# Moving steps and V loads inside the blocks of a fused windowed-attention and SwiGLU kernel, and splitting its last store

## The chip, the core and the metric

The kernel runs on one core of one Trainium2 chip. The metric is the device time in microseconds of one execution, as the median of several runs. TensorE (PE) multiplies matrices and writes PSUM; VectorE (DVE), ScalarE (ACT) and GpSimd (POOL) do the elementwise work; GpSimd also issues most loads, and SyncE (SP) issues the stores and the transposing DMAs. Each engine works through its own list of instructions in order and waits on semaphores for the others.

## What is computed

Attention over 4 batches, 8 heads, 768 positions and a head dimension of 64, in which a query sees the first 8 keys (global) and the 96 keys up to itself (local), with a bias that falls linearly with distance; then a SwiGLU feed-forward over the 3072 tokens, from 512 to 1536 features and back:

```python
scores = scale * np.matmul(q, k.transpose(0, 1, 3, 2))
keep = is_global | is_local
scores = np.where(keep, scores + bias, -1e9)          # bias = -slope_h * distance
a = softmax(scores)
x = np.matmul(a, v)                                   # -> tokens x 512
g = x @ w_gate
out = (g * sigmoid(g)) * (x @ w_val) @ w_out          # float32
```

## The kernel before

Tokens are cut into 8 tiles of 384 (t = 0 to 7), two for each batch, and the 1536 hidden features into 12 slices of 128 (f = 0 to 11). For each (t, f) the feed-forward makes a **gate** group and a **value** group of four matmuls each (L477, `gps` and `vps`), whose results rotate through three PSUM banks. ScalarE takes tanh of half the gate (`th`, L488); VectorE forms `sl` = (th + 1) * gate (L490) and then `hT` = value * `sl` (L494). A bank is free again once `sl`, for a gate, or `hT`, for a value, has read it. The product with `wo` (L506, `ops`) of an earlier tile is cut into **output** groups of three matmuls, of which one is put behind most (t, f); after the fourth, ScalarE copies the 128 x 512 result to `osb` (L511) and SyncE stores it (L513).

The attention of the batch that comes next is put between these groups as **steps**. A step holds some of these:

- `sc(b, hp, bk)`: scores of one pair of heads and one bank of keys (L358), their exponentials on ScalarE (L367), and a multiplication by a mask that holds window and bias (L375, L378; on VectorE, on GpSimd for a few).
- `va(b, hp, half)`: denominators and numerators (`nd`, L406), a copy of the numerators (`ns`, L419), the inversion of the denominators on VectorE (`dT`, `dR`, `rb`, L422 to L427), and the scaled result `xT` (L434), on GpSimd from batch 1 on. `xT` is what the feed-forward reads.
- `fetch`: for batches 2 and 3, SyncE turns keys and queries of two pairs of heads by transposing DMAs (L446) into `kN` and `qT`. `sp` (`spread_keys`, L450) then copies `kN` to the key layout `kT` on VectorE (L454, L457, L458).

Work after the matmuls of a step is not emitted with it but put on the list `later`; one entry is taken off with each following group (L738), all of them before the next step (L745), and also all of them at f = 0 of a token tile (L737).

The steps are dealt out by a count. The program is cut into seven **stretches**; stretch 2 holds the first attention of batch 1, stretches 3 and 4 are the long blocks of two token tiles each (24 f), in which the second half of batch b and the first of batch b + 1 are done in 11 steps, and stretch 5 holds the rest of batch 3. Every group adds its weight (1 for gate or value, 1.1 for output), times a quota, to a debt; when the debt reaches 1, a step is emitted:

```python
        work = sum(g[0] for g in groups)
        quota = len(steps) / (work - (1.0, 0, 5.0, 3.0, 3.0, 4.5, 3.0)[n])
        owed = -0.1 if n == 0 else 0.4
```

The larger the number taken off `work`, the earlier all steps of the stretch come.

Loads of queries, keys and values for later batches are issued by GpSimd, one by one, at places given as 12 t + f (`at_step`, L695). For batches 2 and 3 they are `load_rows` (L196: 16 loads of keys and queries for each batch) and then `load_v_rest` (L171: 7 chunks c of values). Chunks 0 to 3 are read by the first half of a batch's `va`, chunks 3 to 6 by the second.

Of the kernel before, what the change touches and what calls it, by code (L numbers as in the profile page):

```python
# [9 lines left out]
FP32 = mybir.dt.float32  # L10
# [27 lines left out]
def kernel(  # L38
# [12 lines left out]
    nc = tc.nc  # L51
# [7 lines left out]
    DM = H * D  # L59
    DFF = moe_w_gate.shape[1]  # L60
    NFF = DFF // 128
    NC = DM // 128
    J = S // 128
    NCH = 7
# [26 lines left out]
    sb2 = ctx.enter_context(tc.tile_pool(name="sb2", bufs=2))  # L91
# [16 lines left out]
    for hp in range(2):  # L108
        for st, src in ((k32, k), (q32, q)):
            nc.sync.dma_start(  # L110
                out=st[:, 2 * hp:2 * hp + 2, :],
                in_=src[0, 2 * hp:2 * hp + 2, 0:TB, :].rearrange(
                    "h (p j) d -> p h (j d)", p=128))
# [29 lines left out]
    for j in range(J2):  # L143
        nc.vector.tensor_copy(
            out=perm[:, j, :, NG + j::J2],
            in_=identx.rearrange("p (c m) -> p c m", c=NC0))
        n = (NG - j + J2 - 1) // J2
        nc.vector.tensor_copy(
            out=perm[:, j, :, j:NG:J2],
            in_=identx[:, 0:n].unsqueeze(1).broadcast_to([128, NC0, n]))  # L150
# [18 lines left out]
    def load_v_rest(b, c):  # L169
        n = min(KC, S - KC * c)  # L170
        nc.gpsimd.dma_start(  # L171
            out=vSs[b][NG:NG + n, c, :, :],
            in_=v[b, :, KC * c:KC * c + n, :].rearrange("h p d -> p h d"))
# [16 lines left out]
    def stage_rows(b):  # L190
        qst[b] = sb2.tile([128, NP, J, 2, D], FP16, name="qst", tag="qst")
        kst[b] = sb2.tile([128, NP, J, 2, D], FP16, name="kst", tag="kst")

    def load_rows(b, i, h):
        st, src = ((qst[b], q), (kst[b], k))[i]
        nc.gpsimd.dma_start(  # L196
            out=st[:, h // 2, :, h % 2, :],
            in_=src[b, h].rearrange("(t p) d -> p t d", p=128))
# [37 lines left out]
    def single(name, tag, dt=FP32):  # L236
        return ps.tile([128, 512 if dt == FP32 else 1024], dt, name=name, tag=tag)
# [8 lines left out]
    def run_later(n):  # L246
        for _ in range(n):
            if later:
                later.pop(0)()
# [232 lines left out]
    def gate_or_val(t, f, which, c0=0):  # L482
        products(t, f, which, c0, NC)
        dst = gv.pop((f, which))

        if which == 0:
            th = sb2.tile([128, TB], FP32, name="th", tag="th")
            nc.scalar.activation(out=th, in_=dst[:, 0:TB], func=AF.Tanh, scale=0.5)  # L488
            sl = sb2.tile([128, TB], FP32, name="sl", tag="sl")
            nc.vector.scalar_tensor_tensor(  # L490
                out=sl, in0=th, scalar=1.0, in1=dst[:, 0:TB], op0=AluOp.add, op1=AluOp.mult)
            gv["sl"] = sl
        else:
            nc.vector.tensor_mul(hTs[t][:, f, :], dst[:, 0:TB], gv["sl"])  # L494
# [3 lines left out]
    def out_part(t, i, part):  # L498
        if part == 0:
            if t == NT - 1 and i < 2:  # L500
                ops_t[0] = single("ops", f"a{i}")
            else:
                ops_t[0] = single("ops", "o0")
        ops = ops_t[0]
        for f in range(3 * part, 3 * part + 3):
            nc.tensor.matmul(  # L506
                ops, lhsT=hTs[t][:, f, 128 * i:128 * i + 128], rhs=wo[:, f, :],
                start=(f == 0), stop=(f == NFF - 1))
        if part == 3:
            osb = sb2.tile([128, DM], FP32, name="osb", tag="osb")  # L510
            nc.scalar.mul(out=osb, in_=ops, mul=0.5)  # L511
            r0 = TB * t + 128 * i
            nc.sync.dma_start(out=out[r0:r0 + 128, :], in_=osb)  # L513


    NT = TOK // TB
# [178 lines left out]
    def at_step(t, f, *fns):  # L695
        loads.setdefault((t, f), []).extend(fns)
# [12 lines left out]
        at_step(0 if c < 2 else 1, (10 + c) % 12, lambda c=c: load_v_rest(1, c))  # L709
    for c in range(4, NCH):  # L710
        at_step(1, 2 * c - 1 if c < 6 else 10, lambda c=c: load_v_rest(1, c))
    for b, base, rate in ((2, 23, 2.0), (3, 43, 1.4)):
        items = [lambda b=b: stage_rows(b)]
        for hp in range(NP):
            for i in (1, 0):
                for hi in range(2):
                    items.append(lambda b=b, i=i, h=2 * hp + hi: load_rows(b, i, h))
        items += [lambda b=b, c=c: load_v_rest(b, c) for c in range(NCH)]
        for n, it in enumerate(items):
            at_step((base + int(n / rate)) // NFF, (base + int(n / rate)) % NFF, it)  # L720

    outs = [(t, i, part) for t in range(NT - 1) for i in range(3) for part in range(4)]
    for n, (tiles, steps) in enumerate(stretches):
        groups = []
        for t, f, n_out in tiles:
            for which in range(0 if f is None else 2):
                groups.append((0.05 if t == 0 and f < 2 else 1.0, t, f, which))
            groups += [(1.1, t, f, 2)] * n_out
        work = sum(g[0] for g in groups)
        quota = len(steps) / (work - (1.0, 0, 5.0, 3.0, 3.0, 4.5, 3.0)[n])  # L730
        owed = -0.1 if n == 0 else 0.4
        for w, t, f, which in groups:
            if which == 0:
                for ld in loads.pop((t, f), []):
                    ld()
                if f == 0:
                    run_later(len(later))  # L737
            run_later(1)  # L738
            if which == 2:
                out_part(*outs.pop(0))  # L740
            else:
                gate_or_val(t, f, which, NC if t == 0 and f < 2 else 0)
            owed += w * quota
            while owed >= 1.0 and steps:
                run_later(len(later))  # L745
                for step in steps.pop(0):
                    step()
                owed -= 1.0
        assert not steps
    assert not later and not loads and not outs  # L750
    for i in range(3):
        for part in range(4):
            out_part(NT - 1, i, part)
# [35 lines left out]
```

## Time and profile before

| | |
|---|---|
| time, median of 3 runs (lowest, highest) | 263.62 us (263.35, 264.06) |
| span of the profiled execution | 262.0 us |
| `th` on ScalarE, `sl` and `hT` on VectorE, one each | 495, 547, 546 ns |
| `xT` on GpSimd, one | 1001 ns |
| V load, issue on GpSimd, one | 888 ns |
| exponentials of 432 columns, one | 538 ns |
| `osb`, one | 598 ns |

The page gives busy time by engine, then the chain of waits that ended last, then the groups of instructions by line. Busy time says which engine is nearest to full; the chain says whose work was last at each moment; the timeline, which lists instructions with their start and duration, says where an engine had to wait, and for whom. For TensorE, whose matmuls overlap, the distance from one start to the next tells more than the busy time.

### The profile page before, as it was taken

What the parts mean: (1) busy time and instruction counts of PE and PEld (TensorE: products, weight loads), DVE (VectorE), ACT (ScalarE), POOL (GpSimd) and SP (SyncE); (2) the same over time, 40 slices, a digit from 0 to 9 for tenths busy, and PEclk for the clock granted to TensorE, in tenths of its full rate; (3) what the DMA queues carried; (4) which work ended last, traced back from release to release, by engine and by line L of the source; (5) the groups of instructions that cost most, each with busy time, mean ns of one, the idle gap of its engine ahead of it and who ended that gap; (6) DMA issues with size and microseconds to landing.
All of it is one profiled execution on the core that took longest, in us unless ns stands there. A gap on an engine that the chain in (4) does not pass through costs nothing.

```text
span 262.0 us, 5568 instructions
## 1 busy us (share of the span) xinstructions
PE 246.9 (94%) x2144; PEld 140.4 (54%) x2144; DVE 184.1 (70%) x422; ACT 134.7 (51%) x296; POOL 100.8 (38%) x117
## 2 busy tenths in 40 slices
PE   7787899899999999899999999999999999999993
PEld 5464455465655566445555566455565565555541
DVE  6378689967777677987876668977966559656510
ACT  4465687559873564455633653556534643332321
POOL 9663662100236956901338876801111223300000
PEclk9999999999999999999999999999999999999999
DMA  6999999980155999990059996991011101101122
GB/s 164 170 198 166 186 204 203 195 54 3 45 73 62 123 163 112 168 152 13 29 73 79 152 168 60 123 158 43 0 40 44 40 3 40 40 3 40 40 83 80
DMA packets 81010, 24.82 MB, mean 95 GB/s; under 512 B 66832, under 2 KB 77912, under 8 KB 80984
## 3 DMA queue, kind: packets, MB, share of 16 engines
q0 software_dynamic: 63264, 13.83, 60.1%
q1 hardware_dynamic: 17720, 10.64, 18.6%
q8 instruction: 17, 0.28, 0.4%
q14 instruction: 9, 0.07, 0.1%
HBM read 28.63 MB, written 6.29 MB: 133 GB/s over the span
## 4 chain that ended last, share of the span: by engine, by line
PE 68%; DVE 13%; DMA 8%; ACT 4%; issue 3%; POOL 2%; POOLq 0%; DVEq 0%; ACTq 0%
PE ops L506 20%; PE vps L477 19%; PE gps L477 18%; DMA q<-in_q_dram 8%; PE nd L406 6%; PE sc L358 3%; DVE sl L490 3%; DVE hT L494 2%; DVE rb L427 2%; DVE dT L422 2%; ACT at L367 2%; PE trs L262 1%; ACT th L488 1%; DVE dR L423 1%; POOL k L116 1%
## 5 line engine op out<-in xcount | busy, mean ns | idle before, releaser
L488 ACT ACTIVATE th<-gps 128x384 f32<-128x384 f32 x94 | 46.5, 495 | 67.1 <-PE gps L477 63.6
L490 DVE SCALAR_TENSOR_TENSOR sl<-th,gps 128x384 f32<-128x384 f32 x94 | 51.4, 547 | 40.0 <-ACT th L488 39.6
L477 PE MATMUL vps<-xT,wv 128*128 128x384 f16 x376 | 76.6, 326 | 2.0 <-DVE sl L490 1.6
L477 PE MATMUL gps<-xT,wg 128*128 128x384 f16 x376 | 77.0, 327 | 1.3 <-DVE hT L494 0.8
L506 PE MATMUL ops<-wo,hT 128*128 128x512 f16 x288 | 75.7, 380 | 0.0
L434 POOL TENSOR_TENSOR xT<-ns,rb 128x384 f16<-128x384 f32 x24 | 24.0, 1001 | 95.9 <-DVE rb L427 91.9
L494 DVE TENSOR_TENSOR hT<-vps,sl 128x384 f16<-128x384 f32 x94 | 51.3, 546 | 6.9 <-PE vps L477 0.6
L477 PEld LDWEIGHTS <-wg 128*128 128x128 f16 x384 | 36.1, 98 | 34.7 <-issue 3.8
L477 PEld LDWEIGHTS <-wv 128*128 128x128 f16 x384 | 36.0, 98 | 28.5 <-issue 5.1
L506 PEld LDWEIGHTS <-hT 128*128 128x128 f16 x288 | 26.9, 98 | 24.9 <-issue 0.9
L367 ACT ACTIVATE at<-sc 128x432 f16<-128x432 f32 x72 | 33.0, 538 | 3.7 <-PE sc L358 3.7
L171 POOL DMA_DIRECT2D vS<-in_v_dram x25 | 22.1, 888 | 7.6 <-DMA wo<-in_moe_w_out_dram 4.9
L511 ACT ACTIVATE osb<-ops 128x512 f32<-128x512 f32 x24 | 14.4, 598 | 19.8 <-PE ops L506 19.8
L419 ACT COPY ns<-nd 128x384 f32<-128x384 f32 x28 | 13.4, 478 | 17.2 <-PE nd L406 16.4
L427 DVE STREAM_TRANSPOSE rb<-dR 128x384 f32<-128x384 f32 x32 | 18.1, 568 | 0.9
L378 DVE TENSOR_TENSOR at<-at,masks 128x864 f16<-128x864 f16 x20 | 14.4, 720 | 3.4 <-ACT at L367 3.2
L422 DVE STREAM_TRANSPOSE dT<-nd 128x384 f32<-128x384 f32 x28 | 16.1, 573 | 0.3 <-PE nd L406 0.3
L343 ACT ACTIVATE at<-sc 128x432 f16<-128x432 f32 (+2 forms) x32 | 11.9, 444 | 5.8 <-PE sc L335 5.8
L406 PEld LDWEIGHTS <-ones 128*64 128x64 f16 x288 | 10.9, 110 | 7.3 <-issue 6.8
L196 POOL DMA_DIRECT2D kst<-in_k_dram x16 | 13.7, 874 | 0.0
L196 POOL DMA_DIRECT2D qst<-in_q_dram x16 | 13.7, 867 | 0.0
L406 PE MATMUL nd<-at,ones 128*64 128x216 f16 (+6 forms) x256 | 13.2, 231 | 0.0
(77 smaller groups left out, 190.1 us busy)
## 6 DMA issues: line engine op xcount, KB each, us to landing
out_dram<-osb SPq DMA_DIRECT2D x24, 256.0 KB, 2.1
vS<-in_v_dram POOLq DMA_DIRECT2D x21, 120.0 KB, 6.7
wg<-in_moe_w_gate_dram POOLq DMA_DIRECT2D x6, 256.0 KB, 8.8
wv<-in_moe_w_val_dram POOLq DMA_DIRECT2D x6, 256.0 KB, 8.7
wo<-in_moe_w_out_dram POOLq DMA_DIRECT2D x3, 512.0 KB, 11.9
kst<-in_k_dram POOLq DMA_DIRECT2D x16, 96.0 KB, 4.2
qst<-in_q_dram POOLq DMA_DIRECT2D x16, 96.0 KB, 5.1
kst<-in_k_dram POOLq DMA_DIRECT2D x2, 384.0 KB, 15.0
```

Source lines behind the costliest of these rows:

```text
L171: nc.gpsimd.dma_start(out=vSs[b][NG:NG + n, c, :, :], in_=v[b, :, KC * c:KC * c + n, :].rearrange("h p d -> p h d"))
L196: nc.gpsimd.dma_start(out=st[:, h // 2, :, h % 2, :], in_=src[b, h].rearrange("(t p) d -> p t d", p=128))
L367: nc.scalar.activation(out=at[:, hi, :], in_=sc[hi][:, 0:BANK], func=AF.Exp, scale=scale)
L406: nc.tensor.matmul(dst[r, o:o + n], lhsT=ones[:, 0:64] if ones_side else vals[:, 2 * hp + hi, :], rhs=self.at[cb][:, hi, col:col + n], sta ...
L422: nc.vector.transpose(dT, den[:, 0:TB])
L427: nc.vector.transpose(rb.rearrange("p (n i) -> p n i", i=32), dR.unsqueeze(2).broadcast_to([128, TB // 32, 32]))
L434: mul_eng.tensor_mul(dst, src, rb)
L477: nc.tensor.matmul(gv[f, which][:, 0:TB], lhsT=w[:, c, 128 * f:128 * f + 128], rhs=x_of(t)[:, c, :], start=(c == 0), stop=(c == NC - 1))
L488: nc.scalar.activation(out=th, in_=dst[:, 0:TB], func=AF.Tanh, scale=0.5)
L490: nc.vector.scalar_tensor_tensor(out=sl, in0=th, scalar=1.0, in1=dst[:, 0:TB], op0=AluOp.add, op1=AluOp.mult)
L494: nc.vector.tensor_mul(hTs[t][:, f, :], dst[:, 0:TB], gv["sl"])
L506: nc.tensor.matmul(ops, lhsT=hTs[t][:, f, 128 * i:128 * i + 128], rhs=wo[:, f, :], start=(f == 0), stop=(f == NFF - 1))
```

## The change

It does three things. The loads of the values of batches 2 and 3 get places of their own: chunks 0 to 3 about where they were, chunks 4 to 6 behind the boundary between the two token tiles of a block, so that they do not lie with the work around it. The numbers taken off `work` grow in stretches 2 to 5, so that the attention steps end sooner in each block. And the last output tile is copied from PSUM in two halves, by ScalarE and VectorE, and stored by two queues, ScalarE's and SyncE's.

```diff
         if part == 3:
             osb = sb2.tile([128, DM], FP32, name="osb", tag="osb")
-            nc.scalar.mul(out=osb, in_=ops, mul=0.5)
             r0 = TB * t + 128 * i
-            nc.sync.dma_start(out=out[r0:r0 + 128, :], in_=osb)
+            if t == NT - 1 and i == 2:
+
+                oB = sb2.tile([128, DM // 2], FP32, name="osb", tag="th")
+                nc.scalar.mul(out=osb[:, 0:DM // 2], in_=ops[:, 0:DM // 2], mul=0.5)
+                nc.vector.tensor_scalar_mul(oB, ops[:, DM // 2:], 0.5)
+                nc.scalar.dma_start(out=out[r0:r0 + 128, 0:DM // 2], in_=osb[:, 0:DM // 2])
+                nc.sync.dma_start(out=out[r0:r0 + 128, DM // 2:], in_=oB)
+            else:
+                nc.scalar.mul(out=osb, in_=ops, mul=0.5)
+                nc.sync.dma_start(out=out[r0:r0 + 128, :], in_=osb)
...
-    for b, base, rate in ((2, 23, 2.0), (3, 43, 1.4)):
-        items = [lambda b=b: stage_rows(b)]
+    for b, base, rate, v_at in ((2, 24, 2.0, (30, 31, 32, 32, 37, 38, 39)), (3, 43, 1.4, (54, 55, 56, 57, 61, 62, 63))):
+        items = [(base, lambda b=b: stage_rows(b))]
+        n = 0
         for hp in range(NP):
             for i in (1, 0):
                 for hi in range(2):
-                    items.append(lambda b=b, i=i, h=2 * hp + hi: load_rows(b, i, h))
-        items += [lambda b=b, c=c: load_v_rest(b, c) for c in range(NCH)]
-        for n, it in enumerate(items):
-            at_step((base + int(n / rate)) // NFF, (base + int(n / rate)) % NFF, it)
+                    items.append((base + n / rate,
+                                  lambda b=b, i=i, h=2 * hp + hi: load_rows(b, i, h)))
+                    n += 1
+        items += [(at, lambda b=b, c=c: load_v_rest(b, c)) for c, at in enumerate(v_at)]
+        for when, it in items:
+            at_step(int(when) // NFF, int(when) % NFF, it)
...
-        quota = len(steps) / (work - (1.0, 0, 5.0, 3.0, 3.0, 4.5, 3.0)[n])
+        quota = len(steps) / (work - (1.0, 0, 6.0, 6.0, 6.0, 6, 3.0)[n])
```

In the places 12 t + f, the V chunks of batch 2 were at 31, 32, 32, 33, 33, 34, 34 and those of batch 3 at 55, 55, 56, 57, 58, 58, 59; the row loads of batch 2 shift by up to one place.

## The prediction

> **What bounds the kernel now.** Read first the page: shares of busy time, then the chain of waits by engine.
>
> ```profile
> PE 246.9 (94%) x2144; PEld 140.4 (54%) x2144; DVE 184.1 (70%) x422; ACT 134.7 (51%) x296; POOL 100.8 (38%) x117
> ...
> PE 68%; DVE 13%; DMA 8%; ACT 4%; issue 3%; POOL 2%; POOLq 0%; DVEq 0%; ACTq 0%
> ```
>
> TensorE is the bound, and the other engines hold 13% of the chain in short pieces. Then the timeline, looking at when each group of matmuls starts. Undisturbed, four gate or value matmuls and three output matmuls each take 0.65 us on the chain ("0.65 PE vps L477 x4"). A group that starts later than its predecessor's start plus 0.65 was kept waiting. From 56 us on, where the changed code begins, I find eight such places:
>
> ```profile
> 83.67 0.32 PE L477 MATMUL gps<-xT,wg 128*128 128x384 f16 x1 [0.17 <-POOL xT L434]
> ...
> 106.81 1.88 POOL L171 DMA_DIRECT2D vS<-in_v_dram  x2
> ...
> 107.59 1.27 DVE L454 COPY kT<-kN 128x720 f16<-128x720 f16 x1
> ...
> 108.69 1.03 POOL L434 TENSOR_TENSOR xT<-ns,rb 128x384 f16<-128x384 f32 x1
> ...
> 108.78 0.98 DVE L457 COPY kT<-kN 128x48 f16<-128x48 f16 x1
> ...
> 110.35 0.81 PE L477 MATMUL gps<-xT,wg 128*128 128x384 f16 x4 [0.83 <-DVE hT L494]
> ...
> 113.32 1.79 ACT L367 ACTIVATE at<-sc 128x432 f16<-128x432 f32 x4
> ...
> 116.34 0.81 PE L477 MATMUL vps<-xT,wv 128*128 128x384 f16 x4 [0.37 <-DVE sl L490]
> ```
>
> ```profile
> 227.08 0.32 PE L477 MATMUL gps<-xT,wg 128*128 128x384 f16 x1 [0.23 <-POOL xT L434]
> ```
>
> The columns are start, duration, engine, line, operation; the bracket is the idle time before it and who ended it. Lost TensorE time, from the starts: A, 83.67 (due 82.85 + 3 x 0.162 = 83.34): 0.33. B, 110.35 and 111.33 (due 109.36 and 111.00): 0.99 + 0.33. C, 168.48 (due 168.17): 0.31. D, 116.34 and 173.49 (due 115.81 and 172.95): 0.53 + 0.54. E, 219.55 (due 219.31): 0.24. F, 227.08 (due 226.69): 0.39. Sum 3.66 us: all that the moved attention steps and loads can win. Behind the last matmul stands the tail: ACT's eviction 257.98 to 258.58, then the store, to 261.96.
>
> **The causes.** A and F: the last scaled attention tile (xT, L434 on GpSimd) is late for the first gate product of the next token tile. B: two VectorE copies of keys (L454 and L457, normally 0.34 and 0.17, here 1.27 and 0.98) run beside GpSimd's V issues and xT, and lose 0.93 + 0.81 = 1.74 us; hT of feed-forward index 9 comes late, and the ring of three PSUM banks stops TensorE. C: the same at 165.75, where L454 takes 1.06. D: the step "sc 1,0; sc 1,1" lies after the last group of a token tile, and f = 0 of the next one flushes the put-off list at once, so four exponentials (1.79 us) stand on ScalarE ahead of tanh. E: VectorE does two softmax inversions in a row ahead of sl.
>
> **What the Trainium skill says.** "SBUF — State Buffer", section "Who interferes with whom": a VectorE copy in a two-port mode and a GpSimd instruction take one shared port pair, whichever starts first, and the other is blocked for the whole instruction; a VectorE operation with two SBUF inputs is blocked only by a GpSimd instruction that reads SBUF. The trace agrees: L457 ends at 109.76, as the xT that began at 108.69 ends; and L378, with two SBUF inputs, takes 1.24 to 1.25 us beside an xT and about 0.60 beside a load alone. It is less clear for loads: L457 and L458 ran at 102.42 and 102.50 beside a q load without loss. "Trainium Kernel Development and Optimization", "Key Constraints": DMAs of several queues share the 16 engines, and issuing from several only saves issue time. The trace fits: a 256 KB store moves at 334 to 384 GB/s, near the same in all four last bursts.
>
> **The change, part by part.**
>
> 1. Steps earlier. A step is taken when 0.4 + quota x work passes its number. Blocks of 24 f have work 48 + 24 x 1.1 = 74.4; quota 11/71.4 = 0.154 becomes 11/68.4 = 0.161, so step 11 comes at 65.9 instead of 68.8 units. Stretch 2 (work 31.2): step 9 at 24.1 instead of 25.0. Stretch 5 (37.2): step 4 at 28.1 instead of 29.4. A unit is about 0.65 us. In the order built, most steps come one group earlier (0.65 us), those from the fifth in a block one to three. No instruction is added. A and F were 0.33 and 0.39 late, less than one group: both go, **0.72**. D: the step moves to after gate f = 11, so its list is worked off over two more groups; only one pair of exponentials (0.95) is left for the flush. tanh of f = 0 waited for four of them (172.26, done 172.64); with one pair fewer it comes up to 0.9 sooner, and sl with it, more than the 0.54 lost: I take **1.0** of 1.07, since a mask or an eviction may still stand between. E: the first inversion starts one group sooner, ahead of sl; I take 0.1 of 0.24.
>
> 2. V loads. GpSimd still issues 14, each about 0.92 (L171's median; the short last chunk 0.65), costing nothing where GpSimd is idle (38% busy). In each block chunks 4 to 6 go behind the boundary; 0 to 3 come before it. But GpSimd runs through its list as fast as its waits allow: the program place is only the earliest neighbour. Block of batch 2, all about 1 us sooner than before: 12 row loads of 0.83 from 83.0 end near 93; the first xT (before at 98.46) 97.4 to 98.4; then k, k, v (2.6) to 101.0; the second xT to 102.0; q, q, v, v, v (4.4) to 106.4; the next xT's 106.4 to 108.4. The second key spread (L454, L457, L458) now follows directly on the last rb, near 106.8 on the old grid, and again meets those xT's: it ends near 108.5, before 109.84, and now stands ahead of sl of f = 9 (0.55), which frees the bank due at 108.25. So B is about 0.8 instead of 1.32: **0.5** won. In the block of batch 3 GpSimd is not behind, but xT begins about 0.15 us after rb ends, so L457 meets it: loss about 0.85 against 0.72. C stays: 0.
> The shift of the early row loads by one f is hidden: the transposes of pairs 0 and 1 were issued at 87.62 to 93.79 and their copies come only at 102.17.
>
> 3. New waits. V chunk 3 of batch 3 would be issued near 164.9; landing took 6.7 to 7.3 us: 171.6 to 172.2, needed near 173.2. Behind it on TensorE would be everything. I cost it at nothing, bound 1 us. Key copies of pair 2: the transpose issued at 162.43 landed at about 170.1, and the copy now wants it near 169.5; behind it on VectorE waits hT of f = 11. Three V loads fewer share the engines with that transpose (6.2 us median over the run): nothing, bound 0.7 us.
>
> 4. Last store. ScalarE's eviction is halved: th (384 columns) 0.495 and osb (512) 0.598 give 0.80 ns per column, so 256 columns take 0.39; VectorE's half stands in no row; between 0.27 (half of hT's 0.55) and 0.55, I take 0.4. It runs beside, so 0.2 is won (its buffer comes from the tanh pool, whose last reader ended at 249.93). The bytes are the same, so the transfer is not shorter; a second queue may cost up to 0.2 or save 0.2: **0.2**, from 0 to 0.4.
>
> Sum: 0.72 + 1.0 + 0.1 + 0.5 + 0.2 = 2.5; 263.62 - 2.5 = **261.1**.
>
> **Rivals.** Full: V loads out of the way let the key spread run undisturbed, all eight gaps close: 3.66 + 0.3 to 0.4, so 259.6. For it: L454 took 0.34 in six of eight uses. Against: xT alone explains C. Given back: with the steps one group closer together VectorE, already 79 to 89% busy between 100 and 120 us, only moves its backlog; A, F and tail win 0.9, half is lost again: 263.2. For it: the copies at 102.17 ran undisturbed beside an issue, so it is their neighbourhood, not the loads as such, that decides, and every step's neighbourhood changes. Against: VectorE's work per block is unchanged and 70% of the span. Slower: a DMA wait ends last in both blocks (V chunk 3 or key transposes late by 1 us), and the spread ahead of sl doubles B and C (1.6 more), against 0.9 + 1.0 won elsewhere: 263.62 + 2.0 + 1.6 - 1.9 = 265.3.
>
> **Chances.** Forecast 0.55, full 0.22, given back 0.14, slower 0.09. The range reaches from the full case to the given-back one, 259.4 to 263.3. 0.3% is 0.8 us: faster is under 262.8, which the forecast and the full case meet, with a little doubt at the forecast's upper edge: 0.77; same 0.14; slower 0.09.
>
> **What would show it.** Right: gate products at the start of token tiles 2 and 7 without a gap behind xT; no value product of f = 1 of tiles 3 and 5 waiting for sl; ScalarE's exponentials there in pairs, not fours; a gap of 0.3 to 0.9 left around f = 10, 11 of tiles 2 and 4, with L454 or L457 near 1 us; time from the last matmul to the end 0.2 shorter. Wrong: L454 at 0.34 throughout (full case), or TensorE waiting for V, or VectorE for kN (slower). A time above 262.8 would refute the reckoning of D, the largest term.

## The result, and the profile after

The changed kernel takes 260.97 us (median of 4 runs, 260.53 to 261.42) against 263.49 us (4 runs, 263.14 to 264.06): a ratio of 0.9902, 95% interval 0.9877 to 0.9927. The forecast was 261.1, in a range of 259.4 to 263.3.

First the page of the changed kernel: busy time by engine, then the chain of waits by engine.

```profile
PE 246.7 (95%) x2144; PEld 140.6 (54%) x2144; DVE 184.7 (71%) x423; ACT 133.9 (52%) x296; POOL 100.5 (39%) x117
...
PE 76%; DVE 10%; DMA 8%; POOL 2%; issue 1%; ACT 1%; DVEq 0%; ACTq 0%; POOLq 0%
```

The busy times are nearly those of before (TensorE 246.9, VectorE 184.1; the largest difference is ScalarE's, 134.7 to 133.9). What changed is who was last: TensorE holds 76% of the chain instead of 68, VectorE 10 instead of 13, ScalarE 1 instead of 4. So waits went, not work.

Then the timeline of the changed kernel around the eight places of the prediction. The columns are those of the prediction.

```profile
81.12 0.99 POOL L434 TENSOR_TENSOR xT<-ns,rb 128x384 f16<-128x384 f32 x1 [0.70 <-DVE rb L427]
...
82.70 0.81 PE L477 MATMUL gps<-xT,wg 128*128 128x384 f16 x4
...
106.44 0.53 DVE L454 COPY kT<-kN 128x720 f16<-128x720 f16 x1
...
106.77 2.02 POOL L434 TENSOR_TENSOR xT<-ns,rb 128x384 f16<-128x384 f32 x2
...
106.89 0.97 DVE L457 COPY kT<-kN 128x48 f16<-128x48 f16 x1
...
108.45 0.81 PE L477 MATMUL vps<-xT,wv 128*128 128x384 f16 x4 [0.65 <-DVE sl L490]
...
111.02 0.95 ACT L367 ACTIVATE at<-sc 128x432 f16<-128x432 f32 x2
...
113.01 0.95 ACT L367 ACTIVATE at<-sc 128x432 f16<-128x432 f32 x2
...
222.52 0.99 POOL L434 TENSOR_TENSOR xT<-ns,rb 128x384 f16<-128x384 f32 x1 [0.81 <-DVE rb L427]
...
223.86 0.81 PE L477 MATMUL gps<-xT,wg 128*128 128x384 f16 x4
```

A and F: xT ends at 82.11 and 223.51, the four gate products start at 82.70 and 223.86 without a bracket: no wait. D: the exponentials come in pairs. B: the key spread still meets an xT (L457 0.97 instead of 0.17), and now a value group (f = 10) waits for the sl behind it.

**Reading the runs.** The stage up to tile 1 took between 52.5 and 54.1 us in the profiled runs below, although no kernel changes its work there; that is over half of the whole effect. And of the kernels below with an interval, only e2_vloads_only and e9_spread_later have one that does not overlap the changed kernel's. So besides the times ("beside" gives the kernel before in the same session) I give, from each trace, the *middle* (start of the gate group of tile 1, f = 2, to the end of the last matmul) and the *tail* (from there to the end of the span), and the lost TensorE time at each place, reckoned as in the prediction and listed from 0.12 us up. Each is one execution, but the middle repeats well: three kernels that differ only behind it (changed, e5 and e12) have 201.64 to 201.66, two others (e4 and e8) 200.88 and 200.91. In e3 and e9 the time under B and C is lost at score matmuls, not at a gate or value group.

| kernel | A | B | C | D | E + F | middle | tail |
|---|---|---|---|---|---|---|---|
| before | 0.33 | 1.32 | 0.31 | 0.53 + 0.54 | 0.24 + 0.39 | 204.21 | 4.07 |
| changed | 0 | 0.82 | 0.23 | 0 | 0 | 201.64 | 3.97 |
| e1_steps_only | 0 | 0.23 | 0.22 | 0 | 0 | 200.88 | 4.05 |
| e2_vloads_only | 0.34 | 0.54 | 0.31 | 0.54 + 0.54 | 0.24 + 0.39 | 203.42 | 4.07 |
| e3_keys_first | 0 | 0.79 | 0.42 | 0 | 0 | 201.88 | 3.95 |
| e4_v_early | 0 | 0.23 | 0.22 | 0 | 0 | 200.88 | 3.96 |
| e5_tail_two_banks | 0 | 0.83 | 0.23 | 0 | 0 | 201.66 | 3.48 |
| e6_v03_back | 0 | 1.20 | 0.22 | 0 | 0 | 201.86 | 3.96 |
| e7_step6_late | 0 | 0.82 + 0.40 | 0.23 | 0 | 0 | 202.12 | 3.97 |
| e8_v_early_tail | 0 | 0.23 | 0.22 | 0 | 0 | 200.91 | 3.48 |
| e9_spread_later | 0 | 0.17 | 0.17 | 0 | 0 | 200.60 | 3.47 |
| e10_steps67_late | 0 | 0.82 + 0.40 | 0.23 | 0.54 + 0.54 | 0 | 203.18 | 3.97 |
| e11_step7_late | 0 | 0.83 | 0.23 | 0.28 + 0.27 | 0 | 202.17 | 3.96 |
| e12_tail_side_by_side | 0 | 0.82 | 0.23 | 0 | 0 | 201.66 | 3.92 |

The changed kernel wins 2.57 us in the middle and 0.10 in the tail. A further 0.12 that it loses at scores near B is in its middle, but is left out of the table.

### The profile page after: what moved, and what is told of

Same layout as the page of the kernel before. It is cut to its first block, busy times and chain, and to the rows that moved or that the text cites. A ratio compares the mean times of both kernels' runs of the same rounds, so it can differ in the third digit from the quotient of the medians.

```text
span 259.1 us, 5560 instructions
## 1 busy us (share of the span) xinstructions
PE 246.7 (95%) x2144; PEld 140.6 (54%) x2144; DVE 184.7 (71%) x423; ACT 133.9 (52%) x296; POOL 100.5 (39%) x117
## 4 chain that ended last, share of the span: by engine, by line
PE 76%; DVE 10%; DMA 8%; POOL 2%; issue 1%; ACT 1%; DVEq 0%; ACTq 0%; POOLq 0%
PE ops L506 23%; PE vps L477 22%; PE gps L477 20%; PE nd L406 6%; DMA q<-in_q_dram 5%; DMA k<-in_k_dram 3%; PE sc L358 3%; DVE sl L490 2%; DVE dT L422 2%; DVE rb L427 1%; DVE hT L494 1%; PE trs L262 1%; DVE xT L434 1%; DVE kT L457 1%; DVE dR L423 1%
## 5 line engine op out<-in xcount | busy, mean ns | idle before, releaser
L477 PEld LDWEIGHTS <-wv 128*128 128x128 f16 x384 | 34.7, 98 | 26.4 <-issue 4.2
L506 PEld LDWEIGHTS <-hT 128*128 128x128 f16 x288 | 27.7, 98 | 25.3 <-issue 0.5
L378 DVE TENSOR_TENSOR at<-at,masks 128x864 f16<-128x864 f16 x20 | 14.3, 714 | 2.1 <-ACT at L367 1.6
```

The costliest lines, as they stand in the source:

```text
L477: nc.tensor.matmul(gv[f, which][:, 0:TB], lhsT=w[:, c, 128 * f:128 * f + 128], rhs=x_of(t)[:, c, :], start=(c == 0), stop=(c == NC - 1))
L506: nc.tensor.matmul(ops, lhsT=hTs[t][:, f, 128 * i:128 * i + 128], rhs=wo[:, f, :], start=(f == 0), stop=(f == NFF - 1))
```

## The experiments

### Which part carries the gain

Steps alone (the kernel before, one line changed):

```diff
-        quota = len(steps) / (work - (1.0, 0, 5.0, 3.0, 3.0, 4.5, 3.0)[n])
+        quota = len(steps) / (work - (1.0, 0, 6.0, 6.0, 6.0, 6, 3.0)[n])
```

> The kernel before with the earlier steps alone; V loads and the last store as before. Theory S (the earlier steps carry the gain): gaps A, D, E and F close, 0.33 + 1.07 + 0.24 + 0.39, and the key spread, now behind rb with V loads and xT beside it, still costs about 0.8 to 1.3 us at B: 261.3 to 261.8. Theory V (the V loads at the boundary are what hurts, and the steps only ride along): B and C stay at 1.3 and 0.3 and the spread in front of sl makes them worse; 262.3 or more.

Measured: 260.43 us (6 runs), ratio 0.9904 (0.9865 to 0.9943). The middle is 3.33 us shorter than before, *more* than with the whole change. A, D, E and F close, as theory S says; B fell to 0.23, not only to 0.8 to 1.3.

V loads alone (the changed kernel with the old quota and the old last store):

```diff
-        quota = len(steps) / (work - (1.0, 0, 6.0, 6.0, 6.0, 6, 3.0)[n])
+        quota = len(steps) / (work - (1.0, 0, 5.0, 3.0, 3.0, 4.5, 3.0)[n])
```

> The kernel before with the moved V loads alone; steps and the last store as before. Theory S: A, D, E, F stay as they are (2.0 us); with two V issues fewer ahead of the second spread it meets only the xT's, loses about 1 us instead of 1.74, and B falls from 1.32 to between 0.1 and 0.6: 262.4 to 262.9. Theory V: B and C close altogether, L454 and L457 near 0.34 and 0.17: 261.9. A third possibility, that xT alone does the blocking and loads none: L457 at 0.98 as before, B unchanged, 263.5.

Measured: 262.74 us (20 runs), ratio 0.9960 (0.9945 to 0.9974). A, D, E and F stand as before to 0.01; B fell to 0.54. This was theory S. But the middle adds up badly: steps alone -3.33, V loads alone -0.79, both -2.57. On top of the steps, the moved loads cost 0.76 us. (The changed load code shifts row loads too: those of batch 2 come up to one place later, those of batch 3 up to one place earlier.)

### Why the V loads cost time beside the steps

Three kernels, the first with the V loads right out of the way:

```diff
-    for b, base, rate, v_at in ((2, 24, 2.0, (30, 31, 32, 32, 37, 38, 39)), (3, 43, 1.4, (54, 55, 56, 57, 61, 62, 63))):
+    for b, base, rate, v_at in ((2, 24, 2.0, (15, 16, 17, 18, 19, 20, 21)), (3, 43, 1.4, (37, 38, 39, 40, 41, 42, 42))):
```

> The changed kernel with the V loads of batches 2 and 3 moved right out of these parts: those of batch 2 to t = 1, f = 3 to 9, those of batch 3 to t = 3, f = 1 to 6. Theory X: xT then follows each rb at once, so the second spread in the first block meets one xT instead of two, as in the second block; B falls from 0.82 to about 0.25, C stays at about 0.23: 260.4. Theory V: the loads do the blocking; L454, L457 and L458 run at 0.34, 0.17, 0.17 and both gaps close: 259.9.

Measured: 259.82 us (4 runs), ratio 0.9869 (0.9824 to 0.9914); B 0.23, C 0.22. The timeline of this kernel shows which theory holds: the spread no longer has a load beside it, and yet one of its copies is blocked.

```profile
105.16 0.30 DVE L454 COPY kT<-kN 128x720 f16<-128x720 f16 x1
105.38 1.03 POOL L434 TENSOR_TENSOR xT<-ns,rb 128x384 f16<-128x384 f32 x1 [1.08 <-ACT at L367]
105.38 0.17 DVE L457 COPY kT<-kN 128x48 f16<-128x48 f16 x1
105.46 0.98 DVE L458 COPY kT<-kN 128x56 f16<-128x56 f16 x1
```

xT alone does it (theory X): L458 takes 0.98 instead of 0.17 and ends as xT ends, and TensorE loses 0.23 behind it. The row loads lie as in the changed kernel, so the 0.76 us between the two middles are the V loads'.

How they cost it shows one spread earlier. The changed kernel:

```profile
100.41 0.96 POOL L171 DMA_DIRECT2D vS<-in_v_dram  x1
...
100.82 0.71 DVE L454 COPY kT<-kN 128x720 f16<-128x720 f16 x1
...
101.37 1.03 POOL L434 TENSOR_TENSOR xT<-ns,rb 128x384 f16<-128x384 f32 x1
101.46 0.99 DVE L457 COPY kT<-kN 128x48 f16<-128x48 f16 x1
```

Chunk 0 stands ahead of the second xT of the block and puts it off into the first key spread. Times from the start of the middle, for the four kernels of this comparison:

| | changed | e1_steps_only | e4_v_early | e6_v03_back |
|---|---|---|---|---|
| second xT begins | 47.84 | 46.90 | 46.91 | 46.91 |
| first spread takes | 1.71 | 1.01 | 1.03 | 1.01 |
| second spread begins | 52.91 | 52.42 | 52.41 | 52.42 |
| third xT begins | 53.24 | 51.47 | 50.55 | 52.31 |
| second spread, start to sl | 1.42 | 1.20 | 1.21 | 2.18 |

Against e4_v_early, sl is 0.71 late in the changed kernel: 0.50 because the second spread begins later, behind the held-up first one, and 0.21 because it takes longer. TensorE loses 0.12 of that at scores, which wait for the inversion between the two spreads (dT), and 0.60 at B. In e1_steps_only, too, only one copy of the second spread is held up: its third xT is all but over when the spread starts, and the fourth meets L458 (0.97).

Then the places of chunks 0 to 3 put back, only 4 to 6 moved:

```diff
-    ... (2, 24, 2.0, (30, 31, 32, 32, 37, 38, 39)), (3, 43, 1.4, (54, 55, 56, 57, 61, 62, 63))
+    ... (2, 24, 2.0, (31, 32, 32, 33, 37, 38, 39)), (3, 43, 1.4, (55, 55, 56, 57, 61, 62, 63))
```

> The changed kernel with V chunks 0 to 3 at the places they had before (31, 32, 32, 33 and 55, 55, 56, 57); chunks 4 to 6 stay moved. Theory Q (GpSimd's queue: what is issued ahead of an xT delays it into the second spread): one issue of 0.9 us fewer stands ahead of the second xT and of the last two in the first block, so both come about 0.9 us sooner and the gap at B falls from 0.82 to 0.2 to 0.4; C stays near 0.23. Rival (moving chunks 4 to 6, not 0 to 3, is what lost time against the steps alone): B stays at 0.8.

Measured: 260.79 us (one run, beside 263.38); B 1.20, worse than 0.82. Theory Q's premise came true and its forecast did not: the last two xT's came 0.93 us sooner in the middle (52.31 instead of 53.24), but the second spread came 0.49 sooner too, because the first was held up less. The timeline of this kernel:

```profile
102.75 2.78 POOL L171 DMA_DIRECT2D vS<-in_v_dram  x3
105.51 1.98 POOL L434 TENSOR_TENSOR xT<-ns,rb 128x384 f16<-128x384 f32 x2
105.62 2.09 DVE L454 COPY kT<-kN 128x720 f16<-128x720 f16 x1
...
108.39 0.81 PE L477 MATMUL vps<-xT,wv 128*128 128x384 f16 x4 [1.03 <-DVE sl L490]
```

The third xT starts 0.11 us before L454 here, and L454 waits out both (2.09 us); in the changed kernel L454 came 0.33 us ahead and lost 0.19. So the queue ahead of xT decides, but not one way: what matters is which of the two engines comes first. The rival, that moving chunks 4 to 6 did the harm, finds no support in GpSimd's list: in e1_steps_only and here three V chunks are issued ahead of the last two xT's and the others behind them. What differs ahead of them is one row load: five loads between the second xT and the third instead of four, and the third begins 0.84 us later. No run moves the row loads alone.

Last, the order on VectorE instead of that on GpSimd:

```diff
-                [va(b, 0, 1), va(b, 1, 1)], [sp(0), va(b, 2, 1), va(b, 3, 1), sp(1)],
+                [va(b, 0, 1), va(b, 1, 1)], [sp(0), sp(1), va(b, 2, 1), va(b, 3, 1)],
```

> The changed kernel with both key spreads of a block put ahead of the two inversions, so that the second no longer follows directly on rb and the start of xT. Theory X (the gaps left at B and C, 0.82 and 0.23 us, come from the second spread meeting the two xT's released by rb): both close or nearly so, 260.0. Rival D (VectorE simply has too much to do in this part, whatever the order): the gap stays between 0.6 and 1.0 in the first block, only elsewhere: 260.9.

Measured: 260.84 us (4 runs), ratio 0.9900 (0.9860 to 0.9939); B 0.79 and C 0.42. As worded, theory X failed: the gaps didn't close. What rival D forecast came in: a gap of 0.6 to 1.0 in the first block, elsewhere, and 260.9. The timeline of this kernel:

```profile
103.22 0.46 DVE L454 COPY kT<-kN 128x720 f16<-128x720 f16 x1
...
105.85 0.56 DVE L422 STREAM_TRANSPOSE dT<-nd 128x384 f32<-128x384 f32 x1
...
106.47 0.34 PE L358 MATMUL sc<-qT,kT 64*128 64x216 f16 x3 [0.62 <-DVE dT L422]
...
107.09 1.98 POOL L434 TENSOR_TENSOR xT<-ns,rb 128x384 f16<-128x384 f32 x2
107.73 1.82 DVE L378 TENSOR_TENSOR at<-at,masks 128x864 f16<-128x864 f16 x1
```

The spread got by with 0.46. Now the scores wait, for the second inversion (dT), which stands behind both spreads. In the second block it is the same (163.28); the changed kernel loses 0.12 at these scores in the first block and nothing in the second. The mask (0.60 when alone), which has two SBUF inputs, meets the same two xT's, but only after the gap, and no matmul waits for it. So the meeting changed its victim on VectorE, and the gap has another cause: the order. How much of it is the first spread, held up here as in the changed kernel (0.72 and 0.98), this run does not tell; nor does it show that VectorE has too much to do whatever the order.

### The gap at the end of a token tile

The sixth step held back to where it was, with the rest as changed:

```diff
-            while owed >= 1.0 and steps:
+            while (owed >= 1.0 and steps
+                   and not (n in (3, 4) and len(steps) == 6 and which != 2)):
```

> The changed kernel with the sixth step of the two long blocks (scores of pair 1) held back to the last group of the first token tile, where it was before. Theory D (four exponentials at once ahead of tanh): ScalarE shows four L367 together there again, a value group waits about 0.5 us for sl in each block, and the time is 1.0 us above the changed kernel: 262.0. Rival (the gap came from the backlog on VectorE that the V loads and spreads left, not from the step's place): no gap of more than 0.2 there, time as the changed kernel's.

Measured: 260.83 us (4 runs), ratio 0.9901 (0.9873 to 0.9929), the middle 0.48 longer than the changed kernel's. Four exponentials stand together, but no group waits at D: theory D failed, and what its rival forecast came in. The 0.40 lost lies earlier, at a value group of f = 11 (first block) that the step's score matmuls had kept apart from its gate. So my account of D was incomplete: it was the step after that I had not looked at. Two more kernels differ only in `len(steps) in (5, 6)` and `in (5,)`:

> The changed kernel with both the sixth and the seventh step of the long blocks held back to the output groups where they were before (end of the first token tile; f = 1 of the second). With the sixth alone held back, four exponentials stood together again, yet no value group waited behind them: the seventh step's matmuls now lay between gate and value of f = 1. Theory N (the gap at D needs both: the late sl, and no attention matmuls to fill in before the value group): about 0.5 us is back at f = 1 of tiles 3 and 5, at least in the block of batch 3. Rival (D came from the backlog on VectorE before it): no gap at f = 1 here either.

> The changed kernel with the seventh step alone held back to the output group of f = 1, the sixth where the change has it. Theory N with both causes independent: two exponentials only stand at the flush, sl comes in time, no gap of more than 0.1 at f = 1. Rival (it is the seventh step's filling alone that closes D, the exponentials don't matter): 0.3 to 0.5 us at f = 1 of tiles 3 and 5.

Measured, one run each: 262.02 and 260.99 us (beside 264.25 for the kernel before). With both held back, 0.54 is back in both blocks, so the place of the steps makes the gap, not a backlog before it; with the seventh alone, 0.28 and 0.27. The timelines in the block of batch 3, first of e10_steps67_late:

```profile
169.06 1.79 ACT L367 ACTIVATE at<-sc 128x432 f16<-128x432 f32 x4
...
172.08 0.81 PE L477 MATMUL vps<-xT,wv 128*128 128x384 f16 x4 [0.37 <-DVE sl L490]
```

and of e7_step6_late, with the seventh step where the change puts it:

```profile
169.05 1.79 ACT L367 ACTIVATE at<-sc 128x432 f16<-128x432 f32 x4
...
171.62 0.45 PE L406 MATMUL nd<-at,ones 128*64 128x216 f16 x8
...
172.58 0.82 PE L477 MATMUL vps<-xT,wv 128*128 128x384 f16 x4
```

The exponentials are as late in both. In e7_step6_late the attention matmuls lie between gate and value, give TensorE 0.96 us of work (171.62 to 172.58), and sl (171.47, 0.55) is done by the time it comes back. Pairs of exponentials alone cut the gap by half (theory N in the strict form and its rival both miss): in e11_step7_late tanh ends at 170.63, but two masks (L375, from 170.28) keep VectorE, and sl begins at 170.88. The filler alone closes it.

### The tail

The timeline of the changed kernel at its end:

```profile
255.25 0.38 ACT L515 ACTIVATE osb<-ops 128x256 f32<-128x256 f32 x1 [1.99 <-PE ops L506]
255.66 0.37 ACTq L517 DMA_DIRECT2D out_dram<-osb  x1
255.66 0.42 DVE L516 TENSOR_SCALAR osb<-ops 128x256 f32<-128x256 f32 x1 [7.79 <-ACT osb L515]
256.12 0.33 SPq L518 DMA_DIRECT2D out_dram<-osb  x1
```

The halves do not run side by side: VectorE's begins when ScalarE's ends, and the trace names that as its releaser. Two kernels give each half a PSUM bank of its own. In the first the left half is computed, evicted and stored first:

```diff
+        for n, tag in enumerate(("o0", "a2")):
+            cols = slice(DM // 2 * n, DM // 2 * n + DM // 2)
+            ops = single("ops", tag)
+            for f in range(NFF):
+                nc.tensor.matmul(
+                    ops[:, 0:DM // 2], lhsT=hTs[t][:, f, 128 * i:128 * i + 128],
+                    rhs=wo[:, f, cols], start=(f == 0), stop=(f == NFF - 1))
...
```

> The changed kernel with the last output tile computed as two halves of 256 columns in two PSUM banks, the left half first, so that its eviction and store lie beside the matmuls of the right. In the changed kernel the VectorE half began only when the ScalarE half ended (255.66 after 255.25 + 0.38), both reading one bank. Theory B (the order within one bank makes the second half wait): from the end of the last matmul to the end of the span 0.4 to 0.7 us less than the 3.9 of the changed kernel; gaps before that unchanged. Rival: the rest is the fixed part of the store, and 24 shorter matmuls take longer than 12: no gain, or 0.3 us lost.

In the second the two loops are exchanged (for f, for n), so that both halves end together:

> The changed kernel with the halves of the last output tile in two PSUM banks, the matmuls of both halves alternating, so that both halves are complete at the same moment. Theory B (VectorE's half waited because both halves lie in one bank): L516's counterpart starts within 0.1 us of the ScalarE half, and from the end of the last matmul to the end of the span it takes 3.5 to 3.6 us instead of 3.97. Rival (what the two-bank run won was the early store of the left half): 3.9.

Measured, one run each: 260.07 us (beside 263.38) and 260.61 (beside 264.25), with tails of 3.48 and 3.92. The timeline of the second kernel:

```profile
254.90 0.38 ACT L530 ACTIVATE osb<-ops 128x256 f32<-128x256 f32 x1 [1.91 <-PE ops L524]
254.96 0.42 DVE L531 TENSOR_SCALAR osb<-ops 128x256 f32<-128x256 f32 x1 [7.36 <-PE ops L524]
255.31 0.41 ACTq L532 DMA_DIRECT2D out_dram<-osb  x1
255.41 0.33 SPq L533 DMA_DIRECT2D out_dram<-osb  x1
```

Now they do run side by side (each half has a tile of its own as well as a bank, so the runs don't tell these two apart), and SyncE's store is issued 0.49 us after the last matmul (254.92) instead of 0.96 (255.16 to 256.12); and yet the tail is only 0.05 shorter. Theory B is right that the halves can then start together, and wrong that this wins time; its rival holds: from the issue on SyncE to the end it takes 3.43 us when both halves move at once (255.41 to 258.84), 2.99 when the left is gone already (255.31 to 258.30 in the first kernel) and 3.01 in the changed kernel, whose left half has a start of 0.46 us. The early store wins, not the second engine; splitting the matmuls costs 0.02.

### Versions that beat both

> The V loads right out of the blocks, as in the run with early V, together with the last tile in two banks. If the parts add: gaps B and C at 0.23 each, none at A, D, E, F, and the tail 0.4 to 0.7 shorter; 259.2 to 259.8, about 1.5 us under the changed kernel. If the early V loads only shift the wait to the start of the blocks: 260.5 or more.

Measured: 260.06 us (6 runs, 259.16 to 261.71), ratio 0.9870 (0.9837 to 0.9903). Middle and tail add as expected (200.91 and 3.48), together 1.22 us less than the changed kernel's. The time is above the expected 259.2 to 259.8, and above the 259.82 of e4_v_early, whose tail is 0.48 longer: medians of so few runs don't resolve this. Its profiled run had one of the longest first stages, 53.99 us.

> The run before it, and the second key spread of a block taken behind the scores and masks of the next step, four groups after the xT that it met (its kN lies in a buffer of its own, so that the next transposes needn't wait). Theory X (the last 0.23 us at B and at C are the spread meeting one xT): L454, L457 and L458 run at 0.34, 0.17 and 0.17, and the two gaps are below 0.1: 0.4 us less than the run before it. Rival (the next operation of VectorE with two SBUF inputs, the mask, meets the same xT, as with the keys first): a gap of 0.2 to 0.5 stays, only behind L378.

The edit is in the steps of the long blocks, with the second `kN` in a buffer that is free after the first stage:

```diff
-                [va(b, 0, 1), va(b, 1, 1)], [sp(0), va(b, 2, 1), va(b, 3, 1), sp(1)],
-                [sc(n, 0, 0), sc(n, 0, 1), fetch(2, 3)], ...
+                [va(b, 0, 1), va(b, 1, 1)], [sp(0), va(b, 2, 1), va(b, 3, 1)],
+                [sc(n, 0, 0), sc(n, 0, 1), sp(1), fetch(2, 3)], ...
...
+            if hp == 1:
+                self.kN = v16[:, 0:4, :].rearrange("r h x -> r (h x)")
```

Measured: 259.80 us (5 runs), ratio 0.9847 (0.9822 to 0.9873), the fastest; the middle 0.31 below the run before it. The second spread runs undisturbed, and the mask meets xT, but late (1.08 instead of 0.60). Of B and C 0.17 each is left, where theory X said below 0.1, and these stand at other places: scores of pair 1, whose weight load at 110.15 waited 0.39 us for the last copy of their keys, which now come later. The rival's gap behind L378 isn't there. Against the changed kernel it is 1.04 in the middle and 0.50 in the tail.

## Why the prediction was right

- **What bounds it, and the ledger of gaps:** right. No work went, only waits, and 2.57 of the 3.66 us were won.
- **A and F, 0.72:** measured 0.33 + 0.39, all of it, for the reason given; no run with the steps alone or with the whole change shows either gap, and the V loads alone leave both.
- **D, 1.0 of 1.07:** all of it won. The reason was half of the truth: the spreading of the exponentials alone is worth half (e11_step7_late), and the next step's matmuls, moved from the output to the gate group of f = 1, would have closed it by themselves. The prediction's step looked at ScalarE's list and not at what TensorE was given to do meanwhile.
- **B, from 1.32 to about 0.8:** measured 0.82, in part by luck. The reckoning of GpSimd's queue gave xT's from 106.4 to 108.4; they ran from 106.77 to 108.79. But the sum booked 0.5 won under the V loads: with the steps alone it would have been 1.09. The V loads' own effect there is +0.59, a cost. And the reckoning looked at the second spread only. The first, which ran undisturbed before, was held up as well (0.71 and 0.99 for two of its copies), put the second off by 0.49, and so made most of that cost. Of the two xT's named, only the first met the spread; the second met the mask (0.94).
- **Row loads, hidden:** not wholly. No key copy waited for a transpose, but one row load more ahead of the last two xT's goes with a start 0.84 later (e6_v03_back beside e1_steps_only).
- **C, unchanged:** 0.31 to 0.23, through L458 instead of L457.
- **E, 0.1 of 0.24:** all 0.24 went; too cautious.
- **New waits, nothing:** none appeared. The key copies of pair 2 took 0.34 at 168.09.
- **Tail, 0.2:** 0.10. The step that failed is "it runs beside": VectorE's half waited for ScalarE's. The Trainium skill, "PSUM — Partial Sum Buffer", section "PSUM bank collisions raise a hardware error", tells that two engines may not read one bank at the same time and that the compiler puts them one after the other; the two halves lay in one bank. The trace agrees (ScalarE's half ends at 255.63, VectorE's begins at 255.66), and with two banks they ran together (254.90 and 254.96). Side by side it would have been 0.15 (3.92 against 4.07): the last store is issued about 0.2 sooner, but takes 0.07 longer to the end of the span than the one whole store before (3.43 against 3.36).

The working gave 2.5 and the medians 2.52. That is closer than the parts deserve, and the closeness is luck: 0.14 too little was booked at E, 0.07 at D and 0.08 at C, against 0.1 too much in the tail, and the two profiled executions differ by 2.83 us, of which 0.15 comes from the first stage (53.68 and 53.53), where nothing was changed. The four runs of either kernel lie up to 0.9 us apart.

## What to carry to other kernels

Where VectorE copies and GpSimd instructions hold each other up (0.98 instead of 0.17 us beside an xT), count what stands in GpSimd's queue ahead of every instruction that somebody waits for, and look at all VectorE operations that may meet it, not only at the last before the gap: here the meeting that cost most lay one spread before the gap. Moving the copies away handed VectorE's wait to the next operation with two SBUF inputs (the mask, 1.82 and 1.08 instead of 0.60); TensorE waited for neither, but it did wait for what the new order had put later. A load without a wait is issued when its engine reaches it, so its place in the program sets its neighbours and not its time: in e4_v_early the load placed at t = 3, f = 1 was issued at 106.36, while TensorE was at t = 2, f = 10. Where TensorE waits for a chain through other engines, other matmuls put between the two ends of the chain can be worth as much as a shorter chain (at D more: all of the 0.54 instead of half). And a change of several parts is worth measuring part by part: here one part took back 0.76 us of what another had won.

## What was not expected of the hardware

A blocked VectorE instruction isn't always next in line. In e6_v03_back L454 waited for two xT's in a row (2.09 us), and in e3_keys_first L378 did (1.82). The Trainium skill, "SBUF — State Buffer", section "Who interferes with whom", speaks of the whole instruction of whoever comes first; here the second GpSimd instruction went ahead of a copy that had been waiting for 0.9 us. And a V load's issue can hold copies up in part: in the changed kernel L457 and L458 took 0.56 and 0.49 us at 158.29 and 158.37, with only a V issue beside them, while L458 took 0.17 at 102.36 beside a q load's.
